# Two batches of attention in plain float32, the first batch's x on GpSimd, four weight blocks staged ahead

## The chip, the cores and the metric

The program runs on one core of a Trainium2 chip. The metric is the device time of one execution in microseconds (us). Five engines work in order, each down its own list of instructions, and wait for one another through semaphores: TensorE (PE), VectorE (DVE), ScalarE (ACT), GpSimd (POOL) and SyncE (SP, which here only starts DMAs).

## The reference

Attention with a feature map, for 4 batches of 8 heads, 576 positions and 64 columns, followed by two feed-forward layers on 2304 tokens:

```python
def phi(x):
    proj = np.einsum('bhsd,df->bhsf', x, w_phi)                     # 128 features
    proj = proj - np.max(np.abs(proj), axis=-1, keepdims=True)
    return np.concatenate([np.exp(proj), np.exp(-proj)], axis=-1)
kv  = np.einsum('bhsf,bhsd->bhfd', phi(k), v);  z = np.sum(phi(k), axis=2)
num = np.einsum('bhsf,bhfd->bhsd', phi(q), kv)
den = np.einsum('bhsf,bhf->bhs', phi(q), z)[..., None] + 1e-06
x = num / den
h = np.maximum(np.maximum(x @ w1, x @ w2), x @ w3) @ w_out
out = prelu(h @ w_in, alpha) @ w_out2
```

## The kernel before

Heads go in pairs: 4 batches of 4 pairs, 16 turns of one loop. A turn i runs two generators in alternation: `keys(pair i)` and `queries(pair i - 1)`. After turn 3, each turn also carries three units of the first feed-forward layer (`layer1`) for the batch that is complete; the rest of the program is feed-forward work alone.

A pair's keys: k is multiplied with `w_phi` into a PSUM bank `pj` (two banks), in two groups of two 128-position tiles and a tail of 64. DVE takes the negated largest magnitude of each row from it (`mx`, line 193). For a group, ACT then makes the features `ke` directly from `pj`, one 128-column activation for each of 4 blocks and 2 signs with `mx` or its negative `my` as bias (lines 216 and 217); for the tail, DVE subtracts into `ppt` (line 197) and ACT makes two activations from that (225). TensorE sums `ke` with v into the bank `kvp` (tag "kv", one bank, line 266). At the end ACT copies it to `kvs` (277), TensorE transposes it into `kvt` (280, the same tag "kv"), and ACT copies that to `kvf` (283).

A pair's queries: the same projection into `pj`, DVE subtracts into `pp` (197), TensorE transposes `pp` into the bank `pt` (328, one bank), ACT makes both signs of the exponential (336, 337). `num` multiplies with `kvf` into `pn` (235) and ACT copies it to `nd` (317). DMAs bring the sums to `dc`, DVE inverts them (350, 351), DMAs write and spread them (`r_d`, `xr`), DVE multiplies (361), and ACT and DVE split the product x into a high and a low part (67, 73).

Where a product isn't plain float32, each operand is split into two parts of type float32r, and three products replace one. Before, batch 0 is plain in all of this (`plain`); batch 1 is plain in the sums over v alone (`plain_kv`); batches 2 and 3 are not plain at all.

The weights of the first layer come as 64-bit floats, 18 blocks of 512 KB. `split_w123` loads one into `wst` (two buffers), converts it with one ACT and four DVE instructions (80 to 88, in `wt`, two buffers) and splits it with one of ACT and one of DVE (67, 73). `CONVERT_IN` says in which turns three blocks are converted.

The order on each engine is made when the program is built: a scheduler takes instructions by priority (`high_priority`: weights lowest in batch 0) by its own estimate of when they are ready. At run time each engine follows its list.

Of the kernel before, what the change touches and what calls it, by code (L numbers as in the profile page):

```python
# [10 lines left out]
F32 = mybir.dt.float32  # L11
F32R = mybir.dt.float32r
U32 = mybir.dt.uint32
# [21 lines left out]
EPS = 1e-6  # L35
XBUFS = (6, 6)
LAG = 1
CONVERT_IN = (0, 2, 3, 4, 5, 6)
SOON, NOW, LATER, LAST = 400, 1000, -100, -200


# [9 lines left out]
def tile_kernel(ctx: ExitStack, tc: tile.TileContext, qT, kT, tails, v, w_phi, w1, w2, w3, w_out, w_in, w_out2, alpha, out):  # L51
# [92 lines left out]
            raws[pair, what] = t  # L144

    def plain(pair):
        return pair[0] == 0

    def plain_kv(pair):
        return pair[0] < 2  # L150
# [1 line left out]
    def split_w123(f, j):  # L152
        if j == 0:
            w.append([])
        t = ring.tile([P, 2, 512], F32R, tag="w", name="w123t")
        w[f].append(t)
        st = ap.tile([P, 1024], U32, tag="kh", bufs=2, name="wst")
        nc.sync.dma_start(st, (w1, w2, w3)[j][f].bitcast(U32))
        wt = ap.tile([P, 512], F32, tag="kl", bufs=2, name="wt")
        yield from from_f64(st, wt)  # L160
        hi_act(t[:, 0], wt)
        yield
        sub(V, t[:, 1], wt, t[:, 0])

    def at_priority(n, steps):
        while True:
# [39 lines left out]
    def exp_keys(pair):  # L206

        ops = features(pair, "k")
        for g, tiles in enumerate(GROUPS):
            pv, mx = project(ops, tiles)  # L210
            my = ap.tile([P, 4], F32, tag="my", bufs=4, name="my")
            V.tensor_scalar(my, mx, -1.0, None, op0=ALU.mult)
            e = ap.tile([P, 1024], F32, tag="e", bufs=2, name="ke")
            ev = e.rearrange("p (a s f) -> p a s f", s=2, f=P)
            for a in range(4):
                A.activation(ev[:, a, 0], pv[:, a], AF.Exp, bias=mx[:, a : a + 1])  # L216
                A.activation(ev[:, a, 1], pv[:, a], AF.Exp, bias=my[:, a : a + 1], scale=-1.0)
            yield tiles, e
        pp = ap.tile([P, 2, P], F32, tag="ppt", bufs=1, name="ppt")
        less_max(*project(features(pair, "t"), (0,)), pp)  # L220
        tail_of[pair] = pp
        e = ap.tile([P, 1024], F32, tag="e", bufs=2, name="ke")[:, :512]
        ev = e.rearrange("p (a s f) -> p a s f", s=2, f=P)
        for i in range(2):
            A.activation(ev[:, :, i], pp, AF.Exp, scale=signs[:, i : i + 1])
        yield (4,), e
# [10 lines left out]
    def keys(pair):  # L237

        rv = raws[pair, "v"]
        if not plain_kv(pair):  # L240
            if not vs:
                vs.extend(ap.tile([P, 5, 3, D], F32R, tag=tag, bufs=1, name=tag) for tag in ("vh", "vl"))
                part = slice(None)
            else:
                part = slice(None, None, 2)
            vh, vl = vs
            hi_act(vh[:, :, part], rv[:, :, part])
            sub(V, vl[:, :, part], rv[:, :, part], vh[:, :, part])
        kvp = bank("kv", 1, "kvp")
        first = True  # L250
        for tiles, e in exp_keys(pair):
            n = len(tiles) * 512
            if plain_kv(pair):
                ops = ((rv, e),)
            else:
                kh = ap.tile([P, 1024], F32R, tag="kh", bufs=2, name="kh")
                kl = ap.tile([P, 1024], F32R, tag="kl", bufs=2, name="kl")
                hi_act(kh[:, :n], e[:, :n])
                sub(V, kl[:, :n], e[:, :n], kh[:, :n])
                ops = ((vh, kh), (vl, kh), (vh, kl))  # L260
            yield
            for i, t in enumerate(tiles):
                for h in range(2):
                    c = slice(i * 512 + h * 256, i * 512 + h * 256 + 256)
                    for x, y in ops:
                        nc.tensor.matmul(
                            kvp[:, h * 256 : h * 256 + 256],
                            x[:, t, h : h + 2].rearrange("p a d -> p (a d)"),
                            y[:, c],
                            start=first,  # L270
                            stop=t == 4 and y is ops[-1][1],
                            skip_group_check=True,
                        )
                        first = False
        yield
        kvs = ap.tile([P, 512], F32, tag="kvs", bufs=1, name="kvs")
        A.activation(kvs, kvp, AF.Copy)
        kvt = bank("kv", 1, "kvt")
        for i in range(4):
            nc.tensor.transpose(kvt[:, i * P : (i + 1) * P], kvs[:, i * P : (i + 1) * P], ident)  # L280
        if plain(pair):
            kvf = ap.tile([P, 2, 2, P], F32, tag=("kvh", "kvl")[pair[1] % 2], bufs=2, name="kvf")
            A.activation(kvf.rearrange("p a b c -> p (a b c)"), kvt, AF.Copy)
            kvs_of[pair] = (kvf,)
            return
        kvh = ap.tile([P, 2, 2, P], F32R, tag="kvh", bufs=2, name="kvh")
        kvl = ap.tile([P, 2, 2, P], F32R, tag="kvl", bufs=2, name="kvl")
        hi_act(kvh.rearrange("p a b c -> p (a b c)"), kvt)
        sub(V, kvl.rearrange("p a b c -> p (a b c)"), kvt, kvh.rearrange("p a b c -> p (a b c)"))
        kvs_of[pair] = (kvh, kvl)  # L290
# [3 lines left out]

    def queries(pair):

        parts = ("q",) if plain(pair) else ("qh", "ql")
        qf = []
        for n, (o, w) in enumerate(CHUNKS):
            qf.append([])  # L300
            for x in parts:
                tag = f"qh{n}" if x != "ql" and pair[1] % 2 * len(x) != 1 else f"ql{n}"
                qf[n].append(ap.tile([P, 2, 2, w], F32 if plain(pair) else F32R, tag=tag, bufs=1, name=x))
        nd = [ap.tile([P, S], F32, tag="nd", bufs=3, name="nd") for _ in range(2)]

        def num(n):
            o, w = CHUNKS[n]
            kv = kvs_of[pair]
            for h in range(2):
                pn = bank("p1", 3, "pn") if plain(pair) else bank("pn", 1, "pn")  # L310
                ops = []
                for s in range(2):
                    q_ = [t[:, h, s] for t in qf[n]]
                    k_ = [t[:, h, s] for t in kv]
                    ops += [(k_[0], x) for x in q_] + [(x, q_[0]) for x in k_[1:]]
                products(pn[:, :w], ops)
                A.activation(nd[h][:, o : o + w], pn[:, :w], AF.Copy)
# [3 lines left out]

        for g, tiles, pp in chain(project_queries(pair), tail()):
            o, w = (0, 2 * P, SM)[g], ST if g == 2 else 2 * P
            pt = bank("pt", 1, "pt")
            for i in range(len(tiles)):
                for h in range(2):
                    c = h * len(tiles) * P + i * P
                    nc.tensor.transpose(pt[:, c : c + P], pp[:, 2 * i + h], ident)
            n = min(g, 1)
            dst = [t[:, :, :, o - CHUNKS[n][0] : o - CHUNKS[n][0] + w] for t in qf[n]]  # L330
            if plain(pair):
                e = dst[0]
            else:
                e = ap.tile([P, 2, 2, 256], F32, tag="qe", bufs=2, name="qe")[:, :, :, :w]
            pv = pt[:, : 256 * len(tiles)].rearrange("p (h s) -> p h s", h=2)[:, :, -w:]
            A.activation(e[:, :, 0], pv, AF.Exp)
            A.activation(e[:, :, 1], pv, AF.Exp, scale=-1.0)
            if not plain(pair):
                (hi_dve if g == 1 else hi_act)(dst[0], e)
                sub(V, dst[1], e, dst[0])  # L340
            yield
            if g != 1:
                num(n)
# [11 lines left out]
        for c in range(2):  # L355
            cs = slice(c * CH, (c + 1) * CH)
            xr = raw_tile()
            for h in range(2):
                r = slice(h * D, (h + 1) * D)
                nc.sync.dma_start(xr[r], rows[h : h + 1, cs].to_broadcast([D, CH]))  # L360
            V.tensor_tensor(xr, nd[0][:, cs], xr, op=ALU.mult)
            xh, xl = x_tiles(c)
            hi_act(xh, xr)
            sub(V, xl, xr, xh)
            res.append((xh, xl))
        xs[pair[0]].append(res)

# [38 lines left out]
    for i, pair in enumerate(pairs):  # L406
        if i + 1 < len(pairs):
            load_pair(pairs[i + 1])
        with tc.high_priority(offset=0 if plain(pair) else SOON if pair[0] == 1 else NOW):
            if pair == (1, 0):  # L410
                hi_dve(wph, wraw)
                sub(V, wpl, wraw, wph)
            run(*([at_priority(LATER, queries(last))] if last else []), keys(pair))
            last = pair
        if i in CONVERT_IN:
            with tc.high_priority(offset=LAST if i < NPAIR - 1 else 0):
                for j in range(3):
                    run(split_w123(len(w) - (j > 0), j))
        u0 = 3 * (i - NPAIR) - LAG
        for u in range(u0, u0 + 3):  # L420
            if u >= 0:
# [291 lines left out]
```

## Time and profile before

| | us |
|---|---|
| median of 3 runs | 939.18 (936.77 to 941.51) |
| the profiled execution | 941.19 |
| its span | 939.4 |
| TensorE busy in the span | 906.3 (96%) |
| VectorE, ScalarE, GpSimd busy | 658.9, 487.0, 155.1 |

Busy time of TensorE counts a matmul from its start to its modelled end, and matmuls overlap: how close it is to its limit is seen from how far apart the starts stand and from the idle time between. A plain float32 matmul shows as two records, a float32r matmul or a transpose as one.

### The profile page before, as it was taken

The numbers are of one execution on the slowest core, as the hardware profiler recorded it, in microseconds if no ns is written. First come the engines' busy times: TensorE is split into PE (matmuls) and PEld (weight loads), VectorE is DVE, ScalarE is ACT, GpSimd is POOL, SyncE is SP. The second block draws the span as 40 slices with busy tenths as digits, with TensorE's granted clock in tenths as the row PEclk, the third lists the DMA queues.
The fourth block names the chain that finished last, engine by engine and source line by source line (L and its number), as shares of the span: only waits on it lengthen the run. The fifth ranks groups of instructions, "written<-read, shape, count | busy, mean of one in ns | idle before, by whom it ended". The sixth has DMA issues, their size and how long they took to land.

```text
span 939.4 us, 18181 instructions
## 1 busy us (share of the span) xinstructions
PE 906.3 (96%) x6730; PEld 881.6 (94%) x6730; DVE 658.9 (70%) x1281; ACT 487.0 (52%) x1148; POOL 155.1 (17%) x197
## 2 busy tenths in 40 slices
PE   8778899999999999999999999999999998999998
PEld 6556799999999999999999999999999998999998
DVE  5788866878888752689888575446544588878782
ACT  6667665867667841334356363335333354444441
POOL 0000000000000000001100013333333353444440
PEclk9998899999999999999999999999999999999999
DMA  8455422322233112566676755444643344444421
GB/s 275 142 160 158 131 66 58 101 90 85 79 87 86 33 40 57 190 180 189 198 222 219 246 168 159 152 145 156 206 146 116 113 124 116 154 139 131 135 70 45
DMA packets 83161, 126.01 MB, mean 134 GB/s; under 512 B 14208, under 2 KB 61952, under 8 KB 83072
## 3 DMA queue, kind: packets, MB, share of 16 engines
q1 hardware_dynamic: 71744, 99.47, 35.6%
q0 software_dynamic: 6720, 20.65, 6.1%
q10 hardware_dynamic: 4608, 4.72, 1.5%
q8 instruction: 53, 0.87, 0.4%
q14 instruction: 36, 0.29, 0.1%
HBM read 86.91 MB, written 35.46 MB: 130 GB/s over the span
## 4 chain that ended last, share of the span: by engine, by line
PE 39%; DVE 5%; DMA 5%; ACT 3%; issue 2%; ACTq 0%; DVEq 0%; SPq 0%
PE p L235 23%; PE acc L632 15%; DMA hr<-h_d 2%; DMA st<-in_w_in 2%; DVE o L73 1%; DMA y_d<-yo 1%; DMA st<-in_w_out 1%; ACT xh L67 1%; DVE xl L73 1%; ACT wt L80 1%; DVE s L572 0%; ACT o L67 0%; DVE wt L88 0%; ACT wq L67 0%; DVE wt L86 0%
## 5 line engine op out<-in xcount | busy, mean ns | idle before, releaser
L235 PE MATMUL p<-xh,w123t 128*128 128x288 f32 x1152 | 241.0, 298 | 1.1 <-DVE s L391 0.8
L235 PE MATMUL p<-xh,wi 128*128 128x288 f32 x1024 | 203.7, 296 | 0.0
L235 PEld LDWEIGHTS p<-xh,w123t 128*128 128x128 f32 x1152 | 187.0, 188 | 2.7 <-DVE s L391 1.3
L632 PE MATMUL acc<-wq,o 128*128 128x256 f32 x1512 | 181.7, 282 | 3.2 <-DVE o L73 2.9
L632 PEld LDWEIGHTS acc<-wq,o 128*128 128x128 f32 x1512 | 179.9, 190 | 4.9 <-DVE o L73 4.5
L235 PE MATMUL p<-xl,w123t 128*128 128x288 f32 x576 | 171.6, 298 | 0.0
L235 PEld LDWEIGHTS p<-xh,wi 128*128 128x128 f32 x1024 | 163.2, 188 | 0.0
L235 PE MATMUL p<-xl,wi 128*128 128x288 f32 x512 | 149.5, 293 | 0.0
L603 DVE SCALAR_TENSOR_TENSOR g<-neg,al,p 128x288 f32<-128x288 f32 x128 | 64.3, 512 | 63.6 <-ACT neg L601 59.9
L235 PEld LDWEIGHTS p<-xl,w123t 128*128 128x128 f32 x576 | 108.2, 188 | 0.3
L604 POOL DMA_DIRECT2D g_d<-g x128 | 69.5, 544 | 208.4 <-DVE g L603 204.7
L235 PEld LDWEIGHTS p<-xl,wi 128*128 128x128 f32 x512 | 97.1, 190 | 0.0
L601 ACT ACTIVATE neg<-p 128x288 f32<-128x288 f32 x128 | 51.0, 407 | 86.2 <-PE p L235 81.9
L395 POOL DMA_DIRECT2D h_d<-ho x12 | 7.3, 611 | 466.0 <-DVE ho L393 466.0
L235 PE MATMUL p<-xh,wo 128*128 128x288 f32 x384 | 77.3, 297 | 1.8 <-ACT xh L67 1.8
L67 ACT ACTIVATE o<-s 128x512 fp32r<-128x512 f32 x72 | 44.3, 629 | 54.3 <-PE acc L632 30.0
L73 DVE TENSOR_TENSOR xl<-xr,xh 128x288 fp32r<-128x288 f32 x96 | 42.2, 455 | 37.2 <-ACT xh L67 33.2
L67 ACT ACTIVATE xh<-xr 128x288 fp32r<-128x288 f32 x96 | 41.6, 449 | 47.4 <-DMA xr<-y_d 33.4
L235 PEld LDWEIGHTS p<-xh,wo 128*128 128x128 f32 x384 | 61.2, 188 | 2.5 <-ACT xh L67 2.5
L216 ACT ACTIVATE ke<-pj,mx 128x128 f32<-128x128 f32 x128 | 49.1, 384 | 21.9 <-DVE mx L193 21.6
L193 DVE TENSOR_REDUCE mx<-pj 128x4 f32<-128x512 f32 (+1 forms) x80 | 50.3, 632 | 14.4 <-PE pj L235 14.4
L73 POOL TENSOR_TENSOR o<-s,o 128x512 fp32r<-128x512 f32 x34 | 49.5, 1459 | 64.3 <-ACT o L67 59.4
(133 smaller groups left out, 1695.7 us busy)
## 6 DMA issues: line engine op xcount, KB each, us to landing
g_d<-g POOLq DMA_DIRECT2D x128, 144.0 KB, 2.2
a<-g_d SPq DMA_DIRECT2D x36, 512.0 KB, 3.8
st<-in_w_out SPq DMA_DIRECT2D x22, 512.0 KB, 4.1
wst<-in_w SPq DMA_DIRECT2D x18, 512.0 KB, 4.4
xr<-y_d SPq DMA_DIRECT2D x64, 144.0 KB, 2.4
st<-in_w_in SPq DMA_DIRECT2D x16, 512.0 KB, 3.9
v<-in_v SPq DMA_DIRECT2D x16, 480.0 KB, 3.8
hr<-h_d SPq DMA_DIRECT2D x48, 144.0 KB, 4.2
```

Source lines behind the costliest of these rows:

```text
L67: A.activation(dst, src, AF.Copy)
L73: eng.tensor_tensor(dst, src, hi.bitcast(F32), op=ALU.subtract)
L80: A.activation(w, high.bitcast(F32), AF.Abs)
L193: V.tensor_reduce(mx, pv, axis=AX.X, op=ALU.max, apply_absolute_value=True, negate=True)
L216: A.activation(ev[:, a, 0], pv[:, a], AF.Exp, bias=mx[:, a : a + 1])
L235: nc.tensor.matmul(dst, x, y, start=i == 0, stop=i == len(ops) - 1, **kw)
L395: (nc.gpsimd if b == B - 1 else nc.sync).dma_start(h_d[f, :, o : o + CH], ho)
L601: A.activation(neg, p, AF.Relu, scale=-1.0)
L603: V.scalar_tensor_tensor(g, neg, al[:, f : f + 1], p, op0=ALU.mult, op1=ALU.add)
L604: nc.gpsimd.dma_start(g_d[f, :, c * CH : (c + 1) * CH], g)
L632: nc.tensor.matmul(acc[i], x, y, start=half == 0 and f == 0 and n == 0 and PLACE[i][1] == 0, stop=half == 1 and f == 3 and n == 2, skip_gr ...
```

## The change

Five edits. (1) `PLAIN = 5`: the projection of the first pair of batch 1 is plain too, and in all of batch 1 the query features, `kvf` and `num` are plain (`plain_kv` where `plain` stood). (2) Keys of batch 0: DVE subtracts into `pp`, as for queries, and ACT makes the features of a group in two instructions of 512 columns. (3) Batch 0's x: the multiplication, the rounding to the high part and the subtraction run on GpSimd. (4) Weight blocks are fetched four ahead, in buffers that later hold `kh` and `qe`; `CONVERT_IN` spreads the 18 blocks over turns 0 to 7 as 2, 1, 2, 1, 3, 3, 3, 3. (5) In batch 0, `kvt` lies in a bank of the tag "p1" (three banks) rather than "kv", and the transposes of the second query group in the bank "pn" rather than "pt".

```diff
-CONVERT_IN = (0, 2, 3, 4, 5, 6)
+PLAIN = 5
+CONVERT_IN = (2, 1, 2, 1, 3, 3, 3, 3)
     def plain(pair):
-        return pair[0] == 0
+        return pair[0] * NPAIR + pair[1] < PLAIN
@@ split_w123
-        st = ap.tile([P, 1024], U32, tag="kh", bufs=2, name="wst")
-        nc.sync.dma_start(st, (w1, w2, w3)[j][f].bitcast(U32))
+        st = fetched.pop(0)
...
         sub(V, t[:, 1], wt, t[:, 0])
+        fetch()
+    fetched, unfetched = [], [x[f] for f in range(NF1) for x in (w1, w2, w3)]
+    def fetch():
+        if unfetched:
+            tag = ("kh", "qe")[len(unfetched) % 2]
+            st = ap.tile([P, 1024], U32, tag=tag, bufs=2, name="wst")
+            nc.sync.dma_start(st, unfetched.pop(0).bitcast(U32))
+            fetched.append(st)
@@ exp_keys
             pv, mx = project(ops, tiles)
+            e = ap.tile([P, 1024], F32, tag="e", bufs=2, name="ke")
+            ev = e.rearrange("p (a s f) -> p a s f", s=2, f=P)
+            if pair[0] == 0:
+                pp = ap.tile([P, 4, P], F32, tag="pp", bufs=2, name="pp")
+                less_max(pv, mx, pp)
+                A.activation(ev[:, :, 0], pp, AF.Exp)
+                A.activation(ev[:, :, 1], pp, AF.Exp, scale=-1.0)
+                yield tiles, e
+                continue
@@ keys
-        kvt = bank("kv", 1, "kvt")
+        kvt = bank("p1", 3, "kvt") if pair[0] == 0 else bank("kv", 1, "kvt")
...
-        if plain(pair):
+        if plain_kv(pair):
@@ queries
-        parts = ("q",) if plain(pair) else ("qh", "ql")
+        parts = ("q",) if plain_kv(pair) else ("qh", "ql")
...
-                pn = bank("p1", 3, "pn") if plain(pair) else bank("pn", 1, "pn")
+                pn = bank("p1", 3, "pn") if pair[0] == 0 else bank("pn", 1, "pn")
...
-            pt = bank("pt", 1, "pt")
+            pt = bank("pn" if pair[0] == 0 and g == 1 else "pt", 1, "pt")
...
-            if not plain(pair):
+            if not plain_kv(pair):
                 (hi_dve if g == 1 else hi_act)(dst[0], e)
                 sub(V, dst[1], e, dst[0])
...
-            V.tensor_tensor(xr, nd[0][:, cs], xr, op=ALU.mult)
+            e = G if pair[0] == 0 else V
+            e.tensor_tensor(xr, nd[0][:, cs], xr, op=ALU.mult)
             xh, xl = x_tiles(c)
-            hi_act(xh, xr)
-            sub(V, xl, xr, xh)
+            if pair[0] == 0:
+                G.tensor_copy(xh, xr)
+            else:
+                hi_act(xh, xr)
+            sub(e, xl, xr, xh)
@@ the loop over pairs
+        for _ in range(4 if i == 0 else 0):
+            fetch()
...
-            if pair == (1, 0):
+            if i == PLAIN - 1:
...
-        if i in CONVERT_IN:
+        for _ in range(CONVERT_IN[i] if i < len(CONVERT_IN) else 0):
             with tc.high_priority(offset=LAST if i < NPAIR - 1 else 0):
-                for j in range(3):
-                    run(split_w123(len(w) - (j > 0), j))
+                n = sum(len(x) for x in w)
+                run(split_w123(n // 3, n % 3))
```

The order moves with it. On ACT, from the copy `kvs` of the first pair on (`q` are query features), before:

```order
L277 ACTIVATE kvs<-kvp 128x512
L216 ACTIVATE ke<-pj,mx 128x128
L283 ACTIVATE kvf<-kvt 128x512
L336 ACTIVATE q<-pt 128x2x256
L337 ACTIVATE q<-pt 128x2x256
L217 ACTIVATE ke<-pj,my 128x128
```

ACT at the same place, now:

```order
L295 ACTIVATE kvs<-kvp 128x512
L227 ACTIVATE ke<-pp 128x4x128
L228 ACTIVATE ke<-pp 128x4x128
L354 ACTIVATE q<-pt 128x2x256
L355 ACTIVATE q<-pt 128x2x256
L68 ACTIVATE w123t<-wt 128x512
L301 ACTIVATE kvf<-kvt 128x512
```

Eight small activations of a key group (six more follow the rows shown) have become two, and they read `pp` in SBUF, not the bank `pj`. On PE, the second pair's keys beside the first pair's queries, before:

```order
L235 MATMUL pn<-q,kvf 128x256 x4
L266 MATMUL kvp<-ke,v 128x256 x4
L235 MATMUL pj<-wraw,k 128x256 x2
L235 MATMUL pj<-wraw,t 128x256
L328 MATMUL pt<-ident,pp 128x128 x4
L328 MATMUL pt<-ident,ppt 128x128 x2
L266 MATMUL kvp<-ke,v 128x256 x3
```

PE there, now:

```order
L298 MATMUL kvt<-ident,kvs 128x128 x4
L284 MATMUL kvp<-ke,v 128x256 x4
L346 MATMUL pt<-ident,ppt 128x128 x2
L253 MATMUL pn<-q,kvf 128x256 x4
L253 MATMUL pj<-wraw,t 128x256
L346 MATMUL pt<-ident,pp 128x128 x4
L253 MATMUL pj<-wraw,q 128x256 x2
```

The tail's transposes (`pt` from `ppt`) came right behind the second group's in the same bank, and now stand ahead of them in another; the next pair's first sums `kvp` follow the transposes `kvt` at once. On POOL, from the end of its set-up, before:

```order
masks.py:199 AFFINE_SELECT ident<-ident 128x128
L395 DMA h_d<-ho 128x288 x12
L604 DMA g_d<-g 128x288 x128
L73 TENSOR_TENSOR o<-s,o 128x512 x2
L73 TENSOR_TENSOR o<-a,o 128x512
```

POOL there, now:

```order
masks.py:199 AFFINE_SELECT ident<-ident 128x128
L380 TENSOR_TENSOR xr<-nd,xr 128x288 x2
L383 CAST xh<-xr 128x288 x2
L74 TENSOR_TENSOR xl<-xr,xh 128x288 x2
L380 TENSOR_TENSOR xr<-nd,xr 128x288
```

POOL had no arithmetic before the last part of the program; now 24 instructions of 288 columns stand first on it.

## Rows read from the trace of the kernel before

**Rows 1.** The page's 40 equal slices: TensorE's busy tenths and granted clock.

```profile
PE   8778899999999999999999999999999998999998
PEclk9998899999999999999999999999999999999999
```

**Rows 2.** Stretches: length, busy us (records) of PE, PEld, DVE, ACT, POOL; PEclk, DMA.

```profile
15.30:99.40 84.10, 68.34 (x324) 54.18 (x325) 67.43 (x151) 61.71 (x166) 0.00 (x0) 0.94 0.51 155
99.40:111.00 11.60, 8.72 (x36) 7.02 (x35) 11.60 (x26) 8.19 (x23) 0.00 (x0) 0.71 0.56 192
111.00:300.00 189.00, 189.00 (x1461) 187.71 (x1460) 147.82 (x295) 130.55 (x334) 0.00 (x0) 1.00 0.29 80
```

**Rows 3.** Timeline, PE: start us, us, line, tiles, records [idle before, releaser]; `kvt`.

```profile
15.34 0.63 PE L280 MATMUL kvt<-ident,kvs 128*128 128x128 f32 x4 [0.78 <-ACT kvs L277]
...
99.42 0.60 PE L280 MATMUL kvt<-ident,kvs 128*128 128x128 f32 x4
```

**Rows 4.** Timeline, all engines: neighbours on ACT, on DVE, and on PE (plain float32).

```profile
7.40 0.37 ACT L216 ACTIVATE ke<-pj,mx 128x128 f32<-128x128 f32 x1
...
7.65 0.38 ACT L217 ACTIVATE ke<-pj,my 128x128 f32<-128x128 f32 x1
...
14.69 0.68 DVE L193 TENSOR_REDUCE mx<-pj 128x4 f32<-128x512 f32 x1
15.29 0.68 DVE L197 TENSOR_TENSOR pp<-pj,mx 128x512 f32<-128x512 f32 x1
...
62.35 1.03 PE L235 MATMUL pj<-wraw,k 128*128 128x256 f32 x4
63.21 0.59 PE L235 MATMUL pj<-wraw,t 128*128 128x256 f32 x2
```

**Rows 5.** Waits of PE from 4 to 112 us: us in total, times, longest.

```profile
PE pt L328 <- ACT q L337: 6.0, 3, 3.4
PE pj L235 <- ACT ke L217: 3.2, 2, 2.9
PE pj L235 <- DVE pp L197: 2.0, 1, 2.0
PE kvp L266 <- ACT ke L217: 1.6, 1, 1.6
...
PE kvp L266 <- ACT kvf L283: 0.9, 1, 0.9
```

**Rows 6.** Timeline, PE: the longest wait of `pj` for `ke`.

```profile
79.68 0.58 PE L235 MATMUL pj<-wph,xhk 128*128 128x256 f32 x1 [2.90 <-ACT ke L217]
```

**Rows 7.** Groups by line and form, 0 to 260 us: busy us, mean ns, idle before.

```profile
L217 ACT ACTIVATE ke<-pj,my 128x128 f32<-128x128 f32 x102 | 39.9, 391 | 4.8 <-DVE my L212 4.8
L193 DVE TENSOR_REDUCE mx<-pj 128x4 f32<-128x512 f32 x50 | 34.1, 686 | 11.2 <-PE pj L235 11.2
L73 DVE TENSOR_TENSOR ql<-qe,qh 128x1024 fp32r<-128x1024 f32 x15 | 18.2, 1216 | 0.1
L88 DVE SCALAR_TENSOR_TENSOR wt<-wst,wt 128x512 uint32<-128x512 uint32 x18 | 12.3, 685 | 0.1
L361 DVE TENSOR_TENSOR xr<-nd,xr 128x288 f32<-128x288 f32 x20 | 9.1, 456 | 10.4 <-DMA xr<-r_d 10.4
L336 ACT ACTIVATE q<-pt 128x512 f32<-128x512 f32 x8 | 4.8, 606 | 1.1 <-PE pt L328 1.0
```

**Rows 8.** Groups of DVE by line, 750 to 925 us, beside GpSimd's work there.

```profile
L569 DVE TENSOR_TENSOR s<-a 128x512 f32<-128x512 f32 x16 | 17.9, 1120 | 0.6
...
L644 DVE TENSOR_TENSOR out<-acc,u 128x256 f32<-128x256 f32 x16 | 6.6, 416 | 0.0
```

**Rows 9.** Tile `o`: GpSimd's instructions, ns least/median/most, first and last start.

```profile
L73 POOL TENSOR_TENSOR o<-s,o x34: 1291/1399/1757, 755.5 to 912.4; 128x512 fp32r<-128x512 f32 x34
```

**Rows 10.** Timeline, 92 to 114 us: the last pair's sums, their x.

```profile
93.77 2.16 SPq L348 DMA_DIRECT2D dc<-nd  x2
...
106.54 0.45 DVE L361 TENSOR_TENSOR xr<-nd,xr 128x288 f32<-128x288 f32 x1
```

More of the change, by code (lines that the diff above doesn't have):

```diff
@@ L210, in exp_keys @@
             pv, mx = project(ops, tiles)
+            e = ap.tile([P, 1024], F32, tag="e", bufs=2, name="ke")
[7 more added lines that the diff above has]
+                continue
             my = ap.tile([P, 4], F32, tag="my", bufs=4, name="my")
             V.tensor_scalar(my, mx, -1.0, None, op0=ALU.mult)
-            e = ap.tile([P, 1024], F32, tag="e", bufs=2, name="ke")
-            ev = e.rearrange("p (a s f) -> p a s f", s=2, f=P)
             for a in range(4):
@@ L302, in queries @@
                 tag = f"qh{n}" if x != "ql" and pair[1] % 2 * len(x) != 1 else f"ql{n}"
-                qf[n].append(ap.tile([P, 2, 2, w], F32 if plain(pair) else F32R, tag=tag, bufs=1, name=x))
+                qf[n].append(ap.tile([P, 2, 2, w], F32 if plain_kv(pair) else F32R, tag=tag, bufs=1, name=x))
         nd = [ap.tile([P, S], F32, tag="nd", bufs=3, name="nd") for _ in range(2)]
@@ L330, in queries @@
             dst = [t[:, :, :, o - CHUNKS[n][0] : o - CHUNKS[n][0] + w] for t in qf[n]]
-            if plain(pair):
+            if plain_kv(pair):
                 e = dst[0]
@@ L408, in tile_kernel @@
             load_pair(pairs[i + 1])
-        with tc.high_priority(offset=0 if plain(pair) else SOON if pair[0] == 1 else NOW):
-            if pair == (1, 0):
+        for _ in range(4 if i == 0 else 0):
+            fetch()
+        with tc.high_priority(offset=(0, SOON, NOW, NOW)[pair[0]]):
+            if i == PLAIN - 1:
                 hi_dve(wph, wraw)
```

## The prediction

> **What bounds the kernel now.** First the page's slices: TensorE is full and at the full clock nearly everywhere except in the first five slices, some 115 us [rows 1]. The stretches say it sharper: from 111 to 300 us TensorE has no idle time and starts 1461 records in 189 us, one every 0.129 us; from 15.3 to 99.4 us it is busy 68 of 84 us at a granted clock of 0.94, and from 99.4 to 111 at 0.71 [rows 2]. So TensorE sets the end from 111 us on, and only two things move the time: TensorE's own work, and what it loses before 111 us.
>
> To count that loss I price work by how far apart starts stand, since busy times overlap. Four plain records of 256 columns take 63.21 - 62.35 = 0.86 us, so a plain matmul of 256 (two records) costs 0.43 [rows 4]; a float32r one of 288 costs the 0.13 of the full stretch [rows 2]. Other widths go by columns: plain 320 0.53, a transpose 0.107, float32r 0.12 at 256 and 0.147 at 320. On DVE, 512 columns cost 15.29 - 14.69 = 0.60 rather than 0.68, and ACT starts its small ones 0.25 apart [rows 4]. A plain pair has 9 projections, 10 sums over v, 8 products in `num` (four each of 256 and 320) and 14 transposes: 3.9 + 4.3 + 1.7 + 2.1 + 1.5 = 13.5 us.
>
> The transposes `kvt` mark the turns. The first starts at 15.34, the fifth (first pair of batch 1) at 99.42, 21 us per turn [rows 3]. TensorE's work from first to fifth, counted down its list with these prices, is 58 us; the time is 84. The other 26 us are lost, and 99.4 to 111 loses some 6 more. Of the 26, the clock explains 0.06 x 84 = 5 [rows 2]; the waits show where the bulk is [rows 5]: `pt` for ACT's `q` 6.0, `pj` for ACT's `ke` 3.2, `kvp` for `ke` 1.6 and for `kvf` 0.9. The rest are short waits.
>
> **The change part by part.**
>
> *Bank of the query transposes (edit 5).* The 6.0 us are a bank conflict: the tail's transposes follow the second group's in the only `pt` bank and wait until ACT has read it, once for 3.4 us [rows 5]. Now those groups lie in two banks, with the tail's transposes placed first. All three waits go. Next late there is `num`, which needs the same two ACT instructions but the new order puts 2.6 us of other TensorE work (a projection and four sums over v) between the transposes and it, against 1 us of ACT work.
>
> *Bank of `kvt` (5).* The next pair's sums had to wait until ACT copied `kvt` out of the shared bank: 0.9 us [rows 5]. That goes too; "p1" has three banks, and nothing else uses them before layer1 but `pn`.
>
> *Key features in batch 0 (2).* Per group, eight ACT instructions (391 ns each, but 0.25 apart: 2.0 us) [rows 4, 7] become two of 512 columns. No such row reads SBUF; the nearest is `q` from PSUM, 606 ns, some 0.5 back to back [rows 7]: 1.0 us for two, between 0.9 and 1.2. DVE pays one subtraction of 512 columns, 0.60 [rows 4], and saves the tiny `my`. ACT gains 1 us per group, 8 us in batch 0, and `pj` is free after DVE instead of after ACT. The 1.6 us of `kvp` waiting for `ke` mostly go. But the long wait of the other kind, 2.90 us [rows 6], is in the first pair of batch 1, which keeps its eight activations: I leave it in.
>
> *Plain batch 1 (1).* `num` costs 4 x 0.43 + 4 x 0.53 = 3.84 instead of 12 x (0.12 + 0.147) = 3.2 us per pair: 0.65 more, four times; one pair's projection, 9 x 0.43 against 27 x 0.12, is 0.65 more. In all TensorE gets 3.3 us more work, on the path. DVE is rid, per pair, of two `ql` of 1.2 us [rows 7], a rounding and smaller pieces: 4 us, which nothing shows in TensorE's time after 111 us, since TensorE has no idle time there.
>
> *x on GpSimd (3).* DVE loses two multiplications (456 ns [rows 7], 0.37 by starts) and two subtractions per pair, ACT two roundings. GpSimd does six instructions of 288 columns. The trace has GpSimd only at 512 columns, 1291 to 1757 ns [rows 9]; by columns 0.73 to 0.99. Its rounding instruction isn't there at all: at least nothing, at most a GpSimd subtraction's 1.76. I take 0.8 for each, 4.8 per pair, far less than a turn. Nobody waits until layer1: the order puts some 11 us of TensorE work between the last pair's sums and its x. Before, that way took from 93.8 to 106.5, 12.8 us, up to the multiplication [rows 10], so a stall of 0 to 3 us remains, as it does today.
>
> The cost is beside it. DVE instructions with both inputs in SBUF stretch next to GpSimd: 1120 ns on average, where the same 512 columns take 685 in the weight conversion; with one input in PSUM they don't (416 for 256) [rows 7, 8]. About half of DVE's time in a turn is weight conversion, so I expect half of GpSimd's 4.8 us to fall on such work: 2 us of DVE per turn in three turns. The Trainium skill ("SBUF — State Buffer", section "Who interferes with whom") says it harder: a VectorE instruction with two SBUF inputs, or a copy, cast or scalar operation in a fast mode, and a GpSimd instruction lock each other out entirely, while reductions never contend. By that rule the weight conversion would be held for as long as GpSimd runs beside it, which is the first rival below; the stretched rows agree with it.
>
> *Four blocks ahead (4).* The DMAs stay 18; four instead of two stand before the third pair's loads on SP. The first block's conversion waits for its landing either way. Its DVE steps now stand ahead of the first query reduction; I count that as nothing, and 1 us if the four blocks delay it.
>
> *The balance.* Down the new lists with these prices, the work between marks is
>
> | turn | PE | DVE | ACT | DVE before | ACT before |
> |---|---|---|---|---|---|
> | 1 to 2 | 13.4 | 11.1 | 10.7 | 9.9 | 15.1 |
> | 2 to 3 | 12.6 | 13.6 | 10.1 | 16.0 | 11.8 |
> | 3 to 4 | 16.0 | 13.9 | 12.7 | 14.6 | 12.8 |
> | 4 to 5 | 13.8 | 12.9 | 12.1 | 14.8 | 14.8 |
>
> TensorE's sum is 55.8. It also does 2.1 us more ahead of the first mark, so that comes at 15.3 + 2.1 = 17.5. Of the 26 us lost I strike 6.0, 0.9, 1.6, 4 of the clock's 5 (the clock fell behind the long gaps) and some 5 of the short waits, as ACT has 9 us less to do: 8 stay. DVE beside GpSimd adds 2. The fifth mark then comes at 17.5 + 55.8 + 10 = 83.3 instead of 99.4: 16 us. From there to saturation 6 us were lost, of it 3.4 by the clock [rows 2] and 2.0 for DVE's `pp` [rows 5]; DVE has 4 us less per pair, and I take back 2.6, which pays for the rest of `num`. Net 16: the profiled execution's 941.2 (span 939.4 and 1.8 around it) would be 925.2. The median of the runs lies 2.0 lower, so I forecast **923.5**.
>
> **The rivals.**
>
> *VectorE becomes the bound.* Every GpSimd microsecond holds DVE: 4.8 on top of 13.5 makes 18.3 per turn in three turns against 14.1 of TensorE, 12.6 more than TensorE's work, of which the forecast's 10 lost us hold about 6. Time about 930. For it: DVE is already level with TensorE in the table. Against: half of DVE's work reads PSUM.
>
> *The waits trade places.* The order is made from estimates, and before, the turns took 1.33 times the largest sum of an engine in each (63 us). If that ratio stays, the new 57 us become 76 and the fifth mark comes at 93.6. Of those 5.8 us `num` takes 2.6: about 936, no measurable change.
>
> *No waits at all.* Fifth mark at 75, 24 us early, and 2 us more than I count behind it: 913.
>
> *The x arrives late, and the kernel is slower.* Twenty GpSimd instructions must be done before TensorE can take the last pair's x; it gets there at about 94. The first pair's sums are done some 4 us ahead of the second mark, at about 29, and with the 12.8 us from sums to x [rows 10] GpSimd can start at 41. At 0.8 us they follow their inputs. Slower than today by over 0.5% needs x at 115, so (115 - 41) / 20 = 3.7 us per instruction; at 4.5 the time would be about 960. The rows say a quarter of that, but the rounding has no row.
>
> **How the numbers follow.** A measurement of this kernel can tell about 0.5% (4.7 us) from no change: faster is below 934.5, slower above 943.9. The forecast (919 to 928) 0.55, VectorE as the bound 0.18, no waits 0.08: faster 0.81. Trading places 0.13: same. Late x 0.06: slower. The range runs from the case without waits, 913, to the one in which the ratio stays, 936; it leaves out the late x and about half of both edge cases.
>
> **What would show it.** Right: the fifth `kvt` at 80 to 87 us; no wait of `pt` for `q`; `kvp` not waiting for `kvf`; granted clock over 0.97 from the first to the fifth mark; from 100 us on again a record every 0.13 us. Wrong: if GpSimd's instructions of 288 columns take well over 1 us, if `wt` on DVE grows past 1 us in most cases, or if TensorE waits for `xh` at the start of layer1. If the fifth mark is early but the end isn't, time was given back in batch 1, where `num` has one `pn` bank and longer products.

## The result

The changed kernel ran at a median of 925.31 us (five runs, 922.40 to 926.42) against 939.73 us for the kernel before beside it (936.77 to 941.51): a ratio of 0.985, interval 0.982 to 0.987. In a later comparison it ran at 923.30 against 939.0: 0.984 (0.982 to 0.985). The forecast was 923.5, the range 913 to 936. The profiled execution took 925.09 us with a span of 923.3, against 941.19 and 939.4: 16.1 us less.

The page of the changed kernel, with the 40 slices for TensorE and its granted clock, answers to [rows 1]:

```profile
PE   8987999999999999999999999999999998999998
PEclk9999999999999999999999999999999999999999
```

Slices 2, 3 and 5 have filled up, slice 4 (69 to 92 us) went from 8 tenths to 7, and the clock is not lowered in any of the first five. The same in stretches (length; busy us and records of PE, PEld, DVE, ACT, POOL; granted clock, DMA share, GB/s), cut where the first and the fifth `kvt` stand, answers to [rows 2]:

```profile
17.70:81.90 64.20, 58.70 (x295) 48.63 (x293) 58.28 (x116) 48.50 (x117) 15.03 (x18) 1.00 0.61 187
81.90:111.00 29.10, 24.18 (x152) 21.61 (x151) 22.14 (x52) 19.87 (x53) 4.71 (x6) 1.00 0.39 117
111.00:300.00 189.00, 188.92 (x1439) 185.31 (x1437) 139.99 (x283) 130.44 (x337) 0.00 (x0) 1.00 0.28 77
```

And the marks themselves, from the timeline (start us, us, line, tiles, records), which answer to [rows 3]:

```profile
17.73 0.60 PE L298 MATMUL kvt<-ident,kvs 128*128 128x128 f32 x4
...
81.92 0.66 PE L298 MATMUL kvt<-ident,kvs 128*128 128x128 f32 x4
```

The first mark is 2.4 us later, the fifth 17.5 us earlier. With TensorE's instructions priced about as in the prediction, counted from each execution's own list (another rounding of the prices moves the work of the whole program by some 2 us and the differences between the kernels by 0.5):

| stretch | before: us | work | lost | now: us | work | lost |
|---|---|---|---|---|---|---|
| start to first mark | 15.3 | 8.5 | 6.8 | 17.7 | 10.6 | 7.2 |
| first to fifth mark | 84.1 | 58.5 | 25.6 | 64.2 | 55.9 | 8.3 |
| fifth mark to 111 us | 11.6 | 5.2 | 6.4 | 29.1 | 23.1 | 5.9 |
| 111 us to the end | 828.4 | 801.9 | 26.5 | 812.3 | 788.0 | 24.3 |
| sum | 939.4 | 874.1 | 65.3 | 923.3 | 877.6 | 45.7 |

TensorE has some 3.5 us more to do and loses 19.6 less, 17.3 of that between the marks. What it still waits for from 4 to 112 us (us in total, times, longest), to be read beside [rows 5]:

```profile
PE p L253 <- POOL xh L383: 3.1, 1, 3.1
PE pj L253 <- ACT ke L235: 3.0, 2, 2.7
PE pj L253 <- DVE pp L208: 1.8, 1, 1.8
PE pj L253 <- DMA k<-in_kT: 1.2, 1, 1.2
PE pt L346 <- DVE pp L208: 0.9, 1, 0.9
...
PE pn L253 <- ACT kvf L301: 0.5, 1, 0.5
PE kvp L284 <- ACT ke L228: 0.3, 1, 0.3
```

No `pt` waits for `q` and no `kvp` for `kvf`. One long wait of `pj` for `ke` is left, and there is a new one, for GpSimd's `xh`.

The prediction read TensorE's waits only. Those of ScalarE from 15 to 112 us in the kernel before begin with a line that it never used:

```profile
ACT wt L80 <- DMA wst<-in_w: 11.3, 8, 2.4
...
ACT wt L80 <- DVE mx L193: 2.5, 1, 2.5
```

and in the changed kernel:

```profile
ACT wt L81 <- DVE w123t L74: 7.6, 9, 3.7
ACT kvs L295 <- PE kvp L284: 4.2, 3, 2.8
```

ScalarE works its list in order. Before, eight times a weight conversion stood at its head waiting for a block to land, 11.3 us in all, with `ke`, `q` and `kvf` behind it. Now it waits for a block once, ahead of the first mark (from 4 to 112 us):

```profile
ACT wt L81 <- DMA wst<-in_w: 0.3, 1, 0.3
```

The conversion still stands at the head of ScalarE's list, though: 7.6 us for VectorE, which has to free `wt`. From 15 to 112 us ScalarE waited 16.3 us ahead of conversions before (11.3 for blocks, 2.5 and 1.8 for VectorE's `mx` and `my`, 0.7 for `wt`), and 7.6 now. So that wait has shrunk by 8.7 us; the rest has changed its name.

### The profile page after: what moved, and what is told of

Same layout as the page of the kernel before. It is cut to its first block, busy times and chain, and to the rows that moved or that the text cites. A ratio compares the mean times of both kernels' runs of the same rounds, so it can differ in the third digit from the quotient of the medians.

```text
span 923.3 us, 18029 instructions
## 1 busy us (share of the span) xinstructions
PE 899.8 (97%) x6689; PEld 876.6 (95%) x6689; DVE 642.5 (70%) x1239; ACT 468.2 (51%) x1084; POOL 173.5 (19%) x221
## 4 chain that ended last, share of the span: by engine, by line
PE 73%; DVE 11%; DMA 8%; issue 3%; ACT 2%; SPq 0%; POOL 0%; ACTq 0%; DVEq 0%; POOLq 0%
PE p L253 43%; PE acc L656 12%; PE kvp L284 6%; PE pn L253 5%; PE pj L253 5%; DVE o L74 2%; DMA st<-in_w_out 2%; DMA y_d<-yo 2%; PE pt L346 2%; DMA hr<-h_d 1%; DVE wt L87 1%; DVE wt L89 1%; ACT o L68 1%; DVE xl L74 1%; DVE s L596 1%
## 5 line engine op out<-in xcount | busy, mean ns | idle before, releaser
L74 DVE TENSOR_TENSOR xl<-xr,xh 128x288 fp32r<-128x288 f32 x88 | 38.8, 455 | 37.2 <-ACT xh L68 32.2
L68 ACT ACTIVATE xh<-xr 128x288 fp32r<-128x288 f32 x88 | 37.8, 444 | 49.5 <-DMA xr<-y_d 34.3
L204 DVE TENSOR_REDUCE mx<-pj 128x4 f32<-128x512 f32 (+1 forms) x80 | 49.8, 627 | 10.6 <-PE pj L253 10.5
L253 PE MATMUL p<-xl,wo 128*128 128x288 f32 x192 | 56.3, 293 | 0.5 <-DVE xl L74 0.3
```

What stands on the lines that cost most here:

```text
L68: A.activation(dst, src, AF.Copy)
L74: eng.tensor_tensor(dst, src, hi.bitcast(F32), op=ALU.subtract)
L204: V.tensor_reduce(mx, pv, axis=AX.X, op=ALU.max, apply_absolute_value=True, negate=True)
L253: nc.tensor.matmul(dst, x, y, start=i == 0, stop=i == len(ops) - 1, **kw)
```

## The experiments

Theory: the gain is the sum of the prediction's terms (banks, wide key features), plain batch 1 is 3.3 us of cost, GpSimd's and the staging's edits are worth nothing. Rival: the staging, which the prediction put at nothing, carries part of what was credited to banks and key features, because all three show as TensorE waiting for ScalarE. Each edit was undone alone; four were also made alone in the kernel before. Differences in us below are differences of ratios times 939. Each ratio has an interval of some 2 to 4.5 us to either side, so a difference of two of them under 3 to 5 us is not told from nothing. A list of waits is of one execution, which can lie 3 to 4 us off the median of its kernel.

**x back on VectorE and ScalarE.**

```diff
-            e = G if pair[0] == 0 else V
+            e = V
...
-            if pair[0] == 0:
-                G.tensor_copy(xh, xr)
-            else:
-                hi_act(xh, xr)
+            hi_act(xh, xr)
```

> The changed kernel with batch 0's x back on VectorE and ScalarE, all else kept. My theory: GpSimd takes 6 us off VectorE (16 instructions of 0.37) but costs it 3.7 us of stretched instructions beside it and TensorE 3.1 us of waiting for the last pair's high part, so undoing it is worth little: 922 to 928, no wait of TensorE for a GpSimd result, fifth mark within 2 us of 81.9. Rival, GpSimd carries a good part of the gain because VectorE has no idle time there: 930 or more, fifth mark at 86 or later. Second rival, it only costs: below 921.

Measured: 925.80 us, ratio 0.987 (0.982 to 0.991), 2 us above the changed kernel and within the error, as the theory has it. The fifth mark is a miss: it stands at 86.5 us, where the theory had it within 2 us of 81.9 and the rival at 86 or later. Batch 0 does take longer this way, and half of that is made up behind the mark, so the fifth mark alone does not tell the time. TensorE's wait for `xh` is gone; others have come, first in the list of its waits from 4 to 112 us:

```profile
PE kvt L298 <- ACT kvs L295: 3.3, 1, 3.3
PE pn L253 <- ACT q L354: 2.3, 2, 1.6
```

So the stall of 3.1 us on GpSimd is not a loss that undoing the edit would save: others of that size take its place.

**One bank for `pt`, and `kvt` in the bank of the sums.**

```diff
-        kvt = bank("p1", 3, "kvt") if pair[0] == 0 else bank("kv", 1, "kvt")
+        kvt = bank("kv", 1, "kvt")
...
-            pt = bank("pn" if pair[0] == 0 and g == 1 else "pt", 1, "pt")
+            pt = bank("pt", 1, "pt")
```

> The changed kernel with one bank for all query transposes and the transposed sums back in the bank of the sums. My theory: the 6 us of waits of the transposes for ScalarE's exponentials and the 0.9 us of the sums for their copy come back, and the lower granted clock behind the long ones costs some 3 us more: 932 to 937, fifth mark at 88 to 93. Rival, those waits came from a loaded ScalarE and not from the bank, and ScalarE now has 9 us less: below 928, hardly any wait of pt for q.

Measured: 931.01 us, ratio 0.992 (0.990 to 0.995), 7 us slower than the changed kernel, 1 us short of the theory's range; the fifth mark is at 89.5 us and the clock is lowered (0.77 from 60 to 75 us), as the theory has them. TensorE's waits, 4 to 112 us, in the profiled execution (927.84 us, 3 us under the median):

```profile
PE pj L253 <- ACT ke L235: 4.3, 1, 4.3
PE pn L253 <- ACT q L354: 3.2, 2, 2.8
PE kvp L284 <- ACT kvf L301: 1.1, 1, 1.1
```

The size is the forecast one (6.0 + 0.9), but of the names only the smaller comes back, `kvp` for `kvf` with 1.1; there is no wait of `pt` for `q`, which is what the rival expected. The order of the program is made anew for each kernel, and the waits for ScalarE now stand under `pn` and `pj`.

**Banks alone, in the kernel before** (the same two lines, the other way round).

> The kernel before with edit 5 alone: transposed sums and second query transposes of batch 0 in other banks. My theory: as undoing it in the changed kernel cost 6 us, alone it brings 4 to 7: 932 to 935. Rival, with ScalarE still waiting for weight blocks the waits for its results stay, at other places: 936 to 940.

Measured: 935.46 us, ratio 0.9955 (0.9932 to 0.9978), 4 us gained, between the theory's range and the rival's. The rival's waits are there: those of `pt` for `q` fall from 6.0 to 1.7 us, those of `pn` for `q` rise from 1.1 to 4.5:

```profile
PE pn L235 <- ACT q L336: 4.5, 4, 1.8
PE pj L235 <- ACT ke L217: 3.7, 1, 3.7
PE kvt L280 <- ACT kvs L277: 3.1, 2, 2.3
...
PE pt L328 <- ACT q L337: 1.7, 1, 1.7
```

The bank of its own has moved much of the wait to `num`, which needs the same `q`. That ScalarE is late with `q` for another reason is the likely cause; in this kernel it still waits 10.1 us for weight blocks:

```profile
ACT wt L80 <- DMA wst<-in_w: 10.1, 11, 2.7
```

**Eight small activations per key group again.**

```diff
-            if pair[0] == 0:
+            if False:
                 pp = ap.tile([P, 4, P], F32, tag="pp", bufs=2, name="pp")
```

> The changed kernel with eight small activations per key group in batch 0 again, read from PSUM, and no subtraction on VectorE. My theory: ScalarE gets 8 us more work, the bank pj is held longer, sums wait for features: 927 to 931, fifth mark at 84 to 88, with waits of pj or kvp for ke of 2 us and more in batch 0. Rival, VectorE is the engine without idle time there and is rid of 8 subtractions of 0.6 us: 920 to 925, fifth mark at 80 or earlier.

Measured: 931.10 us, ratio 0.992 (0.989 to 0.995), 7 us slower than the changed kernel, at the upper end of the theory's range, with the fifth mark at 86.4 us as it has it. Its waits are only just there: `pj` for `ke` 2.0 us in three times, `kvp` for `ke` 0.7. The wide features are worth about the 8 us that they were forecast to take off ScalarE.

**Wide key features alone, in the kernel before.**

```diff
...
+            if pair[0] == 0:
+                pp = ap.tile([P, 4, P], F32, tag="pp", bufs=2, name="pp")
+                less_max(pv, mx, pp)
+                A.activation(ev[:, :, 0], pp, AF.Exp)
+                A.activation(ev[:, :, 1], pp, AF.Exp, scale=-1.0)
+                yield tiles, e
+                continue
...
```

> The kernel before with edit 2 alone (wide key features in batch 0). Theory (ScalarE bounds the turns of batch 0 and is rid of 1 us per group): 933 to 936 us, ratio 0.993 to 0.996. Rival (the waits for the staged weight blocks and for the query bank stay and take it up): 937 to 940.

Measured: 934.89 us, ratio 0.996 (0.995 to 0.998), 3 us gained, half of what undoing it costs, and as the theory has it. ScalarE's waits from 15 to 112 us suggest where the rest went (the profiled execution, 938.55 us, lies 3.7 us over the median):

```profile
ACT wt L80 <- DMA wst<-in_w: 17.5, 11, 3.0
```

With less work of its own, ScalarE waits 6 us longer for blocks (17.5 instead of 11.3).

**Two blocks ahead instead of four, conversion in threes.**

```diff
-CONVERT_IN = (2, 1, 2, 1, 3, 3, 3, 3)
+CONVERT_IN = (3, 0, 3, 3, 3, 3, 3, 0)
...
-            tag = ("kh", "qe")[len(unfetched) % 2]
+            tag = "kh"
...
-        for _ in range(4 if i == 0 else 0):
+        for _ in range(2 if i == 0 else 0):
```

> The changed kernel with two weight blocks in flight in one pair of buffers, converted in turns 0 and 2 to 6, three each, as before. My theory after the first runs: the kernel before had ScalarE wait 11.3 us, eight times, for a block to land, with the activations that TensorE needs queued behind; staging four ahead took that away, and I had counted it at nothing. So undoing it costs 4 to 8 us: 929 to 933, with 6 us and more of waits of the first weight activation for its DMA between 15 and 100 us. Rival, what was predicted: the staging is worth nothing, 923 to 927.

Measured: 930.76 us, ratio 0.990 (0.987 to 0.993), 5 us slower than the changed kernel, as the theory has it. ScalarE waits for blocks again, and TensorE's first wait is for the features behind them:

```profile
ACT wt L81 <- DMA wst<-in_w: 12.8, 6, 3.1
```

```profile
PE kvp L284 <- ACT ke L228: 3.9, 2, 2.7
```

The edit has two sides, how far ahead blocks are fetched and in which turns they are converted, and no run parts them. How many conversions stand ahead of the fifth mark does not explain the loss: 14 here, 15 in the changed kernel.

**Staging alone, in the kernel before.**

```diff
-CONVERT_IN = (0, 2, 3, 4, 5, 6)
+CONVERT_IN = (2, 1, 2, 1, 3, 3, 3, 3)
...
-        st = ap.tile([P, 1024], U32, tag="kh", bufs=2, name="wst")
-        nc.sync.dma_start(st, (w1, w2, w3)[j][f].bitcast(U32))
+        st = fetched.pop(0)
...
+        for _ in range(4 if i == 0 else 0):
+            fetch()
```

> The kernel before with the staging alone (four blocks ahead, spread over turns 0 to 7), nothing else. My theory: ScalarE's 11.3 us of waiting for blocks go, TensorE's waits for q and ke behind it shrink: 3 to 7 us faster than the kernel before, 932 to 936. Rival, the bank and the features decide and the waits only change place: 937 to 941.

Measured: 932.30 us, ratio 0.991 (0.989 to 0.994), 8 us gained: of the edits made alone, the largest gain. ScalarE waits for a block once instead of eight times:

```profile
ACT wt L80 <- DMA wst<-in_w: 1.5, 1, 1.5
```

and TensorE's waits, 4 to 112 us:

```profile
PE pt L338 <- DVE pp L207: 4.3, 3, 2.4
PE pt L338 <- ACT q L347: 3.5, 3, 1.4
...
PE pt L338 <- ACT qe L347: 1.1, 1, 1.1
...
PE pj L245 <- ACT ke L227: 0.3, 1, 0.3
PE kvp L276 <- ACT ke L227: 0.2, 1, 0.2
```

All of TensorE's waits for `ke` together fall from 5.4 to 0.5 us, those for any result of ScalarE from 15.8 to 9.6. Ahead of `pt` TensorE waits no less than before (8.9 us against 6.8), so this is not the bank's gain under another name: it shows as waits for the features, which the prediction gave to the wide activations. Part of the 8 us may come from the other side of the edit: ahead of the fifth mark stand 13 conversions, 16 in the kernel before.

**Batch 1 in float32r as before, in the changed kernel.**

```diff
-PLAIN = 5
+PLAIN = 4
...
-        if plain_kv(pair):
+        if plain(pair):
...
-        parts = ("q",) if plain_kv(pair) else ("qh", "ql")
+        parts = ("q",) if plain(pair) else ("qh", "ql")
```

(and `plain` for `plain_kv` at the three other places of `queries`; with `PLAIN = 4` the rounding and splitting of `wph` also comes one turn earlier than in the kernel before)

> The changed kernel with batch 1 as before: split features, three float32r products in num, split transposed sums. My theory: TensorE has 3.3 us less work, which counts in full behind the fifth mark; VectorE has 4 us more per pair, which shows only in the first turn of batch 1 as 2 to 4 us of waits for pp and for the split: 922 to 927. Rival, the plain batch 1 is what lets TensorE fill up early: 930 or more, and no saturation until 110 us. Second rival, it is pure cost in TensorE work: 920 to 922.

Measured: 920.14 us, ratio 0.9815 (0.977 to 0.986): below the theory's 922 to 927 and in the second rival's range. To see whether it really lies below the changed kernel, both were run again side by side.

> The changed kernel, but with batch 1 in float32r as before (edit 1 undone), once more beside the changed kernel itself on the same chip. Theory (plain batch 1 is TensorE work on the path and buys nothing): 920 to 922 us, ratio 0.980 to 0.983, 3 to 5 us below the changed kernel of the same comparison. Rival (the earlier difference was between chips): within 1.5 us of the changed kernel.

> The changed kernel itself. Both theories: 924 to 926.5 us, ratio 0.983 to 0.987.

Measured: 919.37 us, ratio 0.979 (0.977 to 0.981), and 923.30 us, ratio 0.984 (0.982 to 0.985). Both lie just under their ranges; the gap, 3.9 us, is the expected one, and the intervals do not meet. By the count of the table above, TensorE loses as much in the one (920.2 - 874.1 = 46.1 us) as in the other (923.5 - 877.6 = 45.9): the 3.5 us of work make up the difference of the spans (3.3). This is the fastest of the kernels run.

**Plain batch 1 alone, in the kernel before.**

```diff
+PLAIN = 5
...
-        return pair[0] == 0
+        return pair[0] * NPAIR + pair[1] < PLAIN
...
-        parts = ("q",) if plain(pair) else ("qh", "ql")
+        parts = ("q",) if plain_kv(pair) else ("qh", "ql")
```

(and `plain_kv` for `plain` elsewhere as in the change; the banks of batch 1 stay its own)

> The kernel before with edit 1 alone (the four pairs of batch 1 in plain float32). Theory (3.3 us more TensorE work, nothing in return): no faster than the kernel before, 938 to 943 us, ratio 0.999 to 1.004. Rival (VectorE's 4 us less per pair shorten the waits of the first pair of batch 1): 934 to 937.

Measured: 939.26 us, ratio 1.001 (0.999 to 1.003): no gain, and a cost of some 1 us, less than its 3.5 us of work. Its waits from 4 to 112 us are still long:

```profile
PE pj L236 <- ACT ke L218: 6.8, 4, 2.4
PE pt L329 <- ACT q L338: 4.4, 3, 2.7
```

but counted as above TensorE has lost 35.9 us by 120 us, against 39.0 before: by one execution of each, part of the extra work fills waits. In the changed kernel, with fewer waits, all of it shows in the time.

**Float32r in batch 1, with wide key features in its first pair.** To the edit of the split batch 1 it adds one:

```diff
-            if pair[0] == 0:
+            if pair <= (1, 0):
                 pp = ap.tile([P, 4, P], F32, tag="pp", bufs=2, name="pp")
```

> The changed kernel with batch 1 split as before (the run that gave 920) and with the wide key features of batch 0 in the first pair of batch 1 as well. My theory: the wait of that pair's projection for eight activations (2.7 us in the changed kernel, 0.7 in the split one) goes: 917 to 920, between 0 and 3 us faster than the split one. Rival, VectorE has no room for two more subtractions there: 921 to 924.

Measured: 923.81 us, ratio 0.9815 (0.977 to 0.986), the same ratio as in the first run without it, so the theory's gain did not come. The long wait for `ke` is gone from TensorE's list and the time is not shorter; TensorE's longest wait is again the 3.1 us for GpSimd's `xh`.

The edits side by side, in us (minus is faster):

| edit | alone, in the kernel before | its share in the changed kernel (from undoing it) | forecast |
|---|---|---|---|
| plain batch 1 | +1 | +4 | +0.7 (3.3 of work, 2.6 taken back for VectorE's relief) |
| wide key features | -3 | -7 | about -6.6 (1.6 and 5 of short waits) |
| x on GpSimd | not run | -2, not told from 0 | +2, and 0 to 3 of stall that the sum leaves out |
| four blocks ahead | -8 | -5 | 0 |
| banks | -4 | -7 | -6.9 |
| sum | -14 | -17 | |

The whole change is 14.4 us. Both columns come near it, so the edits may add up; with single shares good to some 3 us, or 5 for x, this is not shown. The 4 us that the forecast put down to the clock stand in no row: no run shows them by themselves.

## Why the prediction came out

*The place.* That only TensorE's work and its losses ahead of 111 us count held: from 111 us TensorE is as full as before, and 17.3 of the 19.6 us lost less are lost less between the first and the fifth mark.

*The marks.* First mark: forecast 17.5, measured 17.73. Work between the marks: 55.8 and 55.9. Lost there: 10 and 8.3. Fifth mark: 83.3 and 81.92. Behind it, gain and loss were to cancel: there TensorE has 4.0 us more to do (811.1 against 807.1) and loses 2.7 less, which gives 1.4 us back.

*The clock.* Granted at 1.00 from 17.7 to 111 us, forecast over 0.97. Before, each lowered stretch came behind a gap of TensorE of 2.0 to 3.4 us (28 to 32, 78 to 86 and 102 to 110 us). The changed kernel still has gaps of 2.67 and 3.12 us, and no lowered clock behind them in this execution; in the second profiled execution of the same kernel the clock was 0.76 from 63 to 70 us, behind the same 2.67 us gap, and 0.97 from the first to the fifth mark, with the same span (923.5 against 923.3). So the sign held in one execution and only just in the other, and what the clock was worth stays open.

*Banks.* The waits of `pt` for `q` and of `kvp` for `kvf` are gone, and undoing the edit costs 7 us, as forecast. The step "All three waits go" is right only together with the others: alone the bank gives 4, and most of the wait moves to `num`, the place that the prediction named as next late.

*Key features.* Forecast: 8 us less for ScalarE, most of it in short waits. Undone it costs 7. The 2.9 us wait in the first pair of batch 1 was left in, and it is there, 2.67 us long, on the timeline:

```profile
62.71 1.13 PE L253 MATMUL pj<-wraw,k 128*128 128x256 f32 x4 [2.67 <-ACT ke L235]
```

*Plain batch 1.* Forecast 3.3 us of work on the path; counted 3.5, measured 3.9 side by side. But the sum also took 2.6 us back behind the fifth mark, because VectorE has 4 us less per pair there, and that term failed. TensorE does lose 2.7 us less behind the mark than before, yet not through this edit: without it, it loses as much in all (46.1 against 45.9), and behind the mark some 6 us less, not more (the two run side by side).

*x on GpSimd.* Forecast 0.8 us per instruction. The 24 instructions by line (busy us, mean ns):

```profile
L380 POOL TENSOR_TENSOR xr<-nd,xr 128x288 f32<-128x288 f32 x8 | 7.9, 993 | 74.5 <-DMA xr<-r_d 64.8 <-ACT ke L243 9.7
L74 POOL TENSOR_TENSOR xl<-xr,xh 128x288 fp32r<-128x288 f32 x8 | 7.3, 912 | 0.4
...
L383 POOL CAST xh<-xr 128x288 fp32r<-128x288 f32 x8 | 4.8, 612 | 0.3
```

20.0 us for 24, 0.83 each. The rounding, which had no row, is the cheapest of the three. The stall of 0 to 3 us at the start of layer1 came out at its upper end, and with it a sign that the prediction itself listed as one of being wrong, TensorE waiting for `xh` there. It was a poor sign: it says nothing about the total, as undoing the edit showed. The timeline shows the last pair's way from the sums to x:

```profile
79.27 0.48 SPq L366 DMA_DIRECT2D dc<-nd  x1
...
88.06 2.38 SPq L378 DMA_DIRECT2D xr<-r_d  x4
...
91.40 1.59 POOL L380 TENSOR_TENSOR xr<-nd,xr 128x288 f32<-128x288 f32 x1 [12.33 <-DMA xr<-r_d]
93.05 0.42 POOL L383 CAST xh<-xr 128x288 fp32r<-128x288 f32 x1
...
93.53 0.40 PE L253 MATMUL p<-xh,w123t 128*128 128x288 f32 x1 [3.12 <-POOL xh L383]
```

From the DMA of the sums to the multiplication 12.1 us, where [rows 10] have 12.8. GpSimd is idle for 12.33 us ahead of it, so a faster GpSimd would not bring this x sooner than by the last two instructions. About 0.8 of the 1.59 us is waiting for VectorE (last section).

*VectorE beside GpSimd.* Forecast 2 us per turn, 6 in all; counted over the instructions that overlap it is 3.7 from 40 to 96 us. VectorE's groups by line and form from 17 to 96 us, in the changed kernel:

```profile
L204 DVE TENSOR_REDUCE mx<-pj 128x4 f32<-128x512 f32 x19 | 12.9, 677 | 3.2 <-PE pj L253 3.2
L89 DVE SCALAR_TENSOR_TENSOR wt<-wst,wt 128x512 uint32<-128x512 uint32 x16 | 11.4, 720 | 0.1
...
L208 DVE TENSOR_TENSOR pp<-pj,mx 128x512 f32<-128x512 f32 x14 | 9.4, 675 | 0.0
L83 DVE TENSOR_SCALAR wt<-wt 128x512 f32<-128x512 f32 x15 | 7.2, 478 | 0.0
```

and in the kernel before, the two weight lines:

```profile
L88 DVE SCALAR_TENSOR_TENSOR wt<-wst,wt 128x512 uint32<-128x512 uint32 x15 | 10.3, 685 | 0.1
...
L82 DVE TENSOR_SCALAR wt<-wt 128x512 f32<-128x512 f32 x14 | 5.9, 423 | 4.1 <-ACT wt L80 4.0
```

The weight steps grow from 685 to 720 ns and from 423 to 478 on average; the instructions that read `pj` in PSUM stay at 675 to 677. So VectorE did not become the bound, though with 58.3 of 64.2 us busy it is close. The rival had every microsecond of GpSimd hold VectorE, 14 us in three turns; held it was for 3.7, because its work on `pj` went on beside GpSimd, a wait lasts only for what is left of the other's instruction, and as often GpSimd was the one that waited (last section).

*Four blocks ahead: the step that failed.* "I count that as nothing, and 1 us if the four blocks delay it" is off by 5 to 8 us. The working looked at the queue of the DMAs and at VectorE, and not at who stood waiting for them: ScalarE, 11.3 us, with the features and the copies of the sums behind it. (The edit also spreads the conversions over other turns; which of its two sides gives the gain stays open.) Why the total is near all the same: the prediction took the 26 us lost as one sum, struck 17.5 of it (the waits by name, the clock, and 5 us of short waits), and put them down to banks and key features. Those waits had two causes at once, the bank or ScalarE's work, and ScalarE's stall on a DMA: staging alone took TensorE's waits for `ke` from 5.4 to 0.5 us, and undoing it brought them from 3.3 to 6.4. Had the change come without the staging, the forecast would have been the same 923.5, and the kernel without it ran at 930.76. That the total is off by only 2 us is partly luck: a gain counted at nothing (5 to 8 us) stands against a return that did not come (2.6) and a clock's share that no run shows (4).

*The median.* The sum gives 941.2 - 16 - 2.0 = 923.2, stated as 923.5. The forecast took off 2.0 us because the profiled execution before lay that far above its median. The one after lies at its median (925.09 and 925.31), and this is the 1.8 us by which the forecast is low.

*The rivals.* VectorE as the bound (930) did not come, nor did the waits trade places (936): 8.3 us are lost where that case needed some 20. The case without waits (913) did not come either; the version with float32r in batch 1, at 919 to 920, is faster by less work and not by fewer waits. The late x (960) was far off: GpSimd took 0.83 us per instruction, where being slower than before needed 3.7.

## What to carry to other kernels

When one engine waits for another, read that other engine's own waits over the same stretch before giving a price to the cause: here TensorE's waits named a bank and ScalarE's features, while ScalarE itself stood for 11.3 us behind weight blocks that had not landed. Fetching further ahead, with the conversions spread out, was worth as much here (5 to 8 us) as the edits on the path, because the consumer sits in an in-order list ahead of work that the critical engine needs. And extra work on the critical engine was cheap only while it had waits to fill: the same 3.5 us cost about 1 in the kernel before and 4 in the changed one.

## What was not expected of the hardware

GpSimd's rounding cast of 288 float32 columns took 421 ns at its shortest, about half of its two-input instructions (793 ns). Longer ones hold a wait for VectorE, and the other way round. From 60 to 62.5 us in the changed kernel:

```profile
60.15 0.68 DVE L87 SCALAR_TENSOR_TENSOR wt<-wst,wt 128x512 uint32<-128x512 uint32 x1
...
60.45 1.03 POOL L380 TENSOR_TENSOR xr<-nd,xr 128x288 f32<-128x288 f32 x1 [1.18 <-DMA xr<-r_d]
...
60.86 1.17 DVE L89 SCALAR_TENSOR_TENSOR wt<-wst,wt 128x512 uint32<-128x512 uint32 x1
...
61.54 0.77 POOL L383 CAST xh<-xr 128x288 fp32r<-128x288 f32 x1
...
61.95 0.64 DVE L83 TENSOR_SCALAR wt<-wt 128x512 f32<-128x512 f32 x1
```

Take from the end of each of the last four its usual time undisturbed (0.79, 0.68, 0.42, 0.41 us). What is left are starts at 60.69, 61.35, 61.89 and 62.18, each some 0.13 us ahead of the end of the record above it (60.83, 61.48, 62.03, 62.31): one engine starts when the other is done. In this trace all 21 instructions of the two that are stretched by more than 0.08 us beside the other (10 of GpSimd, 11 of VectorE) come out so, 0.08 to 0.14 us ahead, and VectorE's instructions that read `pj` in PSUM, the reductions among them, run beside GpSimd at their usual time. The Trainium skill ("SBUF — State Buffer", section "Who interferes with whom") has the two engines exclude each other, reductions excepted; the trace agrees. It cost each side little: GpSimd's 24 instructions took 20.0 us where their shortest times would make 16.1 (8 x (793 + 421 + 793)), and VectorE lost 3.7. But a wait can be long for a single instruction: GpSimd's multiplication at 91.40 (1.59 us) waited through two weight steps of VectorE in a row.
